# Batch 1's q turned in row pairs, and a new order for every engine, in a fused linear attention and gated unit

## The chip, the core and the metric

The kernel runs on one core of a Trainium2 chip. It is compared by the device time of one execution, in microseconds (us); the times shown are medians of several executions. A core has five engines with a queue of instructions each, which run side by side and wait for each other by semaphores: TensorE (PE in the profile; its weight loads are listed apart as PEld), VectorE (DVE), ScalarE (ACT), GpSimd (POOL) and SyncE (SP), which here only issues transfers (DMAs). TensorE reads SBUF, the core's working memory of 128 partitions, and writes PSUM, eight banks of 2 KB per partition, from which VectorE and ScalarE fetch its results.

## The reference, cut to what matters

```python
def _attn_ref(q, k, v, g_norm):                     # q, k, v: (8, 8, 576, 64)
    kv = np.einsum('bhsd,bhse->bhde', k, v)
    out = np.einsum('bhsd,bhde->bhse', q, kv)
    rms = np.sqrt(np.mean(out * out, axis=-1, keepdims=True) + 1e-06)
    return (out / rms * g_norm).astype(np.float32)

def _moe_ref(x, w_val, conv_w, w_out):              # x: (8, 576, 512)
    ...
    for k in range(K):                              # K = 5, causal
        gate_pre += conv_w[k][None, None, :] * xp[:, k:k + S, :]
    gate = 1.0 / (1.0 + np.exp(-gate_pre))
    val = x @ w_val
    return (gate * val @ w_out).astype(np.float32)
```

The attention's output, heads side by side in 512 channels, is the x of the second part. q, k, v and g_norm are float32; the weights of the second part come as float64 (8 bytes a number) and are narrowed to float32 on the chip.

## The kernel before, in words

Everything is float32. The kernel is a list of steps, the text PLAN at its top. A step is a function name with numbers: `val_product 0 1 1` calls val_product(0, 1, 1), where the first number is mostly the batch. The loop at the end of the file (`for step in PLAN.split(";")`) calls them one after the other, each puts its instructions at the end of its engine's queue, and nothing reorders them: PLAN is the order of all engines at once. What stands behind an @ are the numbers of the buffers that the step takes (`new`, L282): a PSUM bank, or a room in SBUF. A buffer can be taken again once its last reader is done.

One batch of 576 tokens goes through these stages. Chunks are 128 tokens; chunk 4 is the tail of 64.

- k and v are loaded (load_half) and multiplied to one 64x64 kv for each head (kv_product, L475, TensorE), which ScalarE copies out of PSUM (kv_half L485 for batch 0, kv_copy L489 for the others).
- q has to stand with head_dim on the partitions (qT). For batches 2 to 7 VectorE turns it in 32x32 blocks (turn_q, L499). For batches 0 and 1, at the start, TensorE does it: load_q_rows (L366) brings all heads in rows, turn_q_rows turns one chunk into a bank, and sort_q copies the bank to qT. For a batch in PAIRED_Q, turn_q_rows makes one 128x128 transpose of two neighbouring tokens' rows at once (L514), and since the two tokens then lie in different halves of the partitions, sort_q needs four copies of 64 partitions for a chunk (L533; two of batch 0's chunks on VectorE, the rest on ScalarE). For a batch not in PAIRED_Q each token block and head half is its own product with the identity, written straight to its half of the partitions (L520; a float32 product is two instructions), and sort_q is a single copy of 128 partitions on ScalarE (L529).
- q times kv gives the raw output (raw_half L562 for batch 0, raw_pair and raw_tail L550 for the others; raw_pair b c makes chunks c and c-1). Its squares are made by ScalarE (square, L595, L599), summed by VectorE (sums, L606), raised to the power -1/2 by GpSimd (powers, L616), and multiplied in (normalise, batch 0 by VectorE at L625, the others by ScalarE at L635 in eight pieces, one for each head).
- For batches 0 and 1 TensorE turns x (turn_x, L647) and ScalarE copies it to xT (keep_x, L654); from batch 2 on VectorE (turn_blocks) and transfers (move_blocks, L668) do it, but for the tail.
- The gate: ScalarE starts it (gate_start, L679), VectorE adds four taps (gate_tap, L685), ScalarE makes the sigmoid (gate_end, L692). The product x @ w_val is val_product (L697, with keep_val L706) for batches 0 and 1; for the later ones it is val_fast (L746), a scheme with seven products in place of eight that needs sums of x (x_sums) and of weights (val_sums) from VectorE. VectorE multiplies gate and value (gated, L710).
- The output product is fast_product (L837) of the same scheme, with token_sums and weight_sums by VectorE, fast_keep to gather it, and store to write it; the tails go by out_product (L784).

The weights are loaded in four blocks each (stage_weight wval 0 to 3, wout 0 to 3, and cw) and narrowed in seven steps (narrow_weight wval 0 5 is step 5 of block 0): 0, 4, 5, 6 and 7 on VectorE (L399, L411, L416, L421, L425), 1, 2 and 3 on ScalarE (L404, L406, L408). val_product b j needs block j of wval. turn_cw (L450) and keep_cw (L454 to L456, VectorE) bring the convolution's weights and g_norm into columns; start_warm (L463) are products on TensorE whose result nobody reads.

Loads go out on SyncE's queue (batch 0's v and half of its q on ScalarE's).

Of the kernel before, what the change touches and what calls it, by code (L numbers as in the profile page):

```python
# [21 lines left out]
stage_weight cw 0 @ 0; turn_q_rows 0 2 @ 1; turn_q_rows 0 4 @ 2; sort_q 0 2 @ 0; turn_q_rows 0 1 @ 3;  # L22
sort_q 0 4; turn_q_rows 0 0 @ 4; turn_q_rows 0 3 @ 5; sort_q 0 1; start_warm 3 256 @ 6; sort_q 0 3;
load_q_rows 1 1; load_q_rows 1 0; stage_weight wval 3; narrow_weight cw 0 5 @ 0; sort_q 0 0;
kv_product 0 0 @ 0 7; narrow_weight cw 0 6 @ 1; narrow_weight cw 0 0 @ 0; start_warm 1 256 @ 2; kv_half 0 0;
narrow_weight cw 0 1; raw_half 0 1 0 @ 1; narrow_weight cw 0 2; kv_product 0 1; narrow_weight cw 0 3;
narrow_weight cw 0 4; narrow_weight cw 0 7; narrow_weight wval 0 5 @ 2; turn_cw @ 3; kv_half 0 1;
load_half k 2 1 @ 0; raw_half 0 3 0 @ 5; narrow_weight wval 0 0 @ 1; narrow_weight wval 0 6 @ 3;
stage_weight wval 2; narrow_weight wval 0 1; raw_half 0 0 1 @ 6; load_half k 1 0; keep_cw; raw_half 0 3 1;
narrow_weight wval 1 0 @ 0; narrow_weight wval 0 2; stage_weight wout 0 @ 1; raw_half 0 2 0 @ 4;  # L30
narrow_weight wval 1 5 @ 0; stage_weight wout 1 @ 2; square 0 3 @ 0; raw_half 0 2 1;
narrow_weight wval 1 6 @ 1; load_half v 1 0; raw_half 0 4 0 @ 2; narrow_weight wval 0 3; sums 0 3 @ 0 0;
load_half k 1 1; raw_half 0 4 1; square 0 2 @ 1; narrow_weight wval 0 4; raw_half 0 0 0; powers 0 3;
narrow_weight wval 1 1; load_half v 1 1; raw_half 0 1 1; narrow_weight wval 0 7; square 0 4 @ 2;
square 0 0 @ 0; sums 0 2; narrow_weight wval 1 2; sums 0 4; load_half k 2 0 @ 0; normalise 0 3 @ 0;
narrow_weight wval 1 3; powers 0 2; sums 0 0; turn_q_rows 1 3 @ 0; square 0 1 @ 1; narrow_weight wval 1 4;
turn_x 0 3 @ 7; narrow_weight wval 3 0 @ 1; sums 0 1; turn_q_rows 1 0 @ 3; keep_x 0 3; load_half v 2 0 @ 0;
# [192 lines left out]
def kernel(  # L230
# [30 lines left out]
    TURNED_X = 2  # L261
    FAST_VAL = 2
    FAST_OUT = 0
    PAIRED_Q = (0,)
    ACT_SUMS = ()
    ROOTS = {(0, 2): H + H // 2, (0, 1): 2 * H}
    GATES = 3
# [646 lines left out]
```

## Time and profile before

| | us |
|---|---|
| median of three runs | 302.18 |
| the runs | 301.41, 302.18, 302.92 |
| the profiled execution | 300.9 |
| its span, first to last instruction | 299.1 |

The profile is that of one execution. A row of the order in time has the start in us, the length, the engine, the line, the operation, the tile written and those read, the shape of a stationary operand (for TensorE) and of out, and how many such instructions are merged in it; in brackets the time the engine stood idle before it and what ended that. A row of a group has busy time, the mean of one instruction in ns, and the idle time before them. A row of a stretch has its two ends and its length, then for each engine the busy time and the number of instructions, the granted TensorE clock (1.00 is full speed), the share of the sixteen DMA engines' time, and GB/s. Busy times of TensorE overlap, since a matmul starts before the one ahead of it has ended; the distance from one start to the next is what an instruction costs there.

### The profile page before, as it was taken

What the parts mean: (1) busy time and instruction counts of PE and PEld (TensorE: products, weight loads), DVE (VectorE), ACT (ScalarE), POOL (GpSimd) and SP (SyncE); (2) the same over time, 40 slices, a digit from 0 to 9 for tenths busy, and PEclk for the clock granted to TensorE, in tenths of its full rate; (3) what the DMA queues carried; (4) which work ended last, traced back from release to release, by engine and by line L of the source; (5) the groups of instructions that cost most, each with busy time, mean ns of one, the idle gap of its engine ahead of it and who ended that gap; (6) DMA issues with size and microseconds to landing.
All of it is one profiled execution on the core that took longest, in us unless ns stands there. A gap on an engine that the chain in (4) does not pass through costs nothing.

```text
span 299.1 us, 8756 instructions
## 1 busy us (share of the span) xinstructions
PE 289.4 (97%) x3333; PEld 226.9 (76%) x3333; DVE 271.8 (91%) x483; ACT 194.9 (65%) x606; POOL 114.2 (38%) x127
## 2 busy tenths in 40 slices
PE   7979999999999999999999999999999999999993
PEld 4666777778887768778788857788887588888582
DVE  2699999999999999999999999999999999999812
ACT  2888898998767957839773666647579343534230
POOL 3047029437478049309740197400593080000000
PEclk9999999999999999999999999999999999999999
DMA  7999795976588747986886669661650063311344
GB/s 267 380 378 413 271 254 156 307 226 206 150 223 208 231 134 152 289 215 159 259 233 220 175 136 293 195 194 52 158 129 14 22 165 70 99 26 46 77 115 124
DMA packets 32073, 55.51 MB, mean 186 GB/s; under 512 B 6166, under 2 KB 14358, under 8 KB 32032
## 3 DMA queue, kind: packets, MB, share of 16 engines
q1 hardware_dynamic: 29520, 49.76, 56.4%
q0 software_dynamic: 1632, 3.17, 4.8%
q10 hardware_dynamic: 880, 2.03, 1.8%
q8 instruction: 26, 0.43, 0.6%
q14 instruction: 15, 0.12, 0.1%
HBM read 39.21 MB, written 9.44 MB: 163 GB/s over the span
## 4 chain that ended last, share of the span: by engine, by line
PE 82%; DVE 9%; DMA 4%; issue 1%; POOL 1%; SPq 1%; ACT 1%; DVEq 0%
PE bank L837 33%; PE bank L746 28%; PE bank L697 6%; PE bank L550 5%; PE bank L784 5%; DMA y<-in_moe_w_val_dram 4%; PE bank L475 4%; DVE gate L685 3%; DVE ss L606 1%; PE bank L647 1%; POOL rt L616 1%; DVE wexp L411 1%; DVE wval L425 1%; ACT x L635 1%; DVE x L625 1%
## 5 line engine op out<-in xcount | busy, mean ns | idle before, releaser
L685 DVE SCALAR_TENSOR_TENSOR gate<-xT,cwT,gate 128x576 f32<-128x576 f32 x128 | 101.2, 807 | 0.9
L616 POOL TENSOR_TENSOR rt<-ss,mhalf 128x8 f32<-128x8 f32 (+3 forms) x38 | 69.6, 1842 | 59.6 <-DVE ss L606 59.5
L635 ACT ACTIVATE x<-bank,rt 128x64 f32<-128x64 f32 x252 | 55.9, 367 | 8.0 <-POOL rt L616 7.9
L668 POOL DMA_DIRECT2D xT<-y x48 | 26.6, 560 | 71.9 <-PE bank L837 38.0
L837 PE MATMUL bank<-wsum,w 128*128 128x256 f32 x192 | 46.8, 382 | 0.0
L837 PEld LDWEIGHTS bank<-wsum,w 128*128 128x128 f32 x192 | 35.8, 190 | 6.3 <-issue 0.8
L746 PE MATMUL bank<-xs,vsum 128*128 128x288 f32 x144 | 38.5, 407 | 0.0
L697 PE MATMUL bank<-xT,wval 128*128 128x288 f32 x128 | 34.0, 414 | 0.0
L746 PEld LDWEIGHTS bank<-xs,vsum 128*128 128x128 f32 x144 | 27.1, 190 | 7.3 <-DVE gv L753 0.2
L837 PE MATMUL bank<-wout,gv 128*128 128x256 f32 x128 | 32.6, 380 | 0.0
L599 ACT ACTIVATE sq<-bank 128x256 f32<-128x256 f32 (+1 forms) x70 | 21.1, 380 | 12.7 <-PE bank L550 12.5
L697 PEld LDWEIGHTS bank<-xT,wval 128*128 128x128 f32 x128 | 23.4, 190 | 6.4 <-ACT xT L654 0.2
L837 PEld LDWEIGHTS bank<-wout,gv 128*128 128x128 f32 x128 | 24.2, 190 | 3.9
L746 PE MATMUL bank<-xT,wval 128*128 128x288 f32 x96 | 26.4, 408 | 0.0
L606 DVE TENSOR_REDUCE ss<-sq 128x8 f32<-128x520 f32 (+1 forms) x40 | 24.8, 627 | 1.6 <-ACT sq L599 1.6
L679 ACT ACTIVATE gate<-xT,cwT 128x576 f32<-128x576 f32 x32 | 25.8, 813 | 0.5 <-DVE gv L710 0.2
L692 ACT ACTIVATE gate<-gate 128x576 f32<-128x576 f32 x32 | 22.2, 709 | 5.1 <-DVE gate L685 5.1
L847 DVE TENSOR_TENSOR ot<-bank,ot 128x512 f32<-128x512 f32 (+1 forms) x32 | 17.0, 547 | 9.0 <-ACT ot L849 4.9
L710 DVE TENSOR_TENSOR gv<-gv,gate 128x576 f32<-128x576 f32 x32 | 23.5, 750 | 0.9 <-ACT gate L692 0.7
L746 PEld LDWEIGHTS bank<-xT,wval 128*128 128x128 f32 x96 | 18.0, 190 | 4.5 <-ACT x L635 0.2
L550 PEld LDWEIGHTS bank<-kv,qT 64*64 64x64 f32 x1008 | 16.3, 135 | 5.7 <-issue 3.9
L475 PEld LDWEIGHTS bank<-v,k 64*64 64x64 f32 x1008 | 16.0, 135 | 3.8 <-issue 1.6
(93 smaller groups left out, 453.4 us busy)
## 6 DMA issues: line engine op xcount, KB each, us to landing
qs<-in_q_dram SPq DMA_DIRECT2D x96, 140.0 KB, 3.9
out_dram<-ot SPq DMA_DIRECT2D x140, 64.0 KB, 1.9
k<-in_k_dram SPq DMA_DIRECT2D x14, 576.0 KB, 4.3
v<-in_v_dram SPq DMA_DIRECT2D x12, 576.0 KB, 6.0
xT<-y SPq DMA_DIRECT2D x48, 64.0 KB, 2.6
xT<-y POOLq DMA_DIRECT2D x48, 64.0 KB, 2.3
y<-in_moe_w_val_dram SPq DMA_DIRECT2D x4, 512.0 KB, 11.5
w<-in_moe_w_out_dram SPq DMA_DIRECT2D x4, 512.0 KB, 9.6
```

Of the source, the lines that this page charges most:

```text
L475: nc.tensor.matmul(st["kvps", b][s][r * D:(r + 1) * D, i], st["k", b, i][rows, r, cols], st["v", b, i][rows, r, cols], start=(j == 0), sto ...
L550: nc.tensor.matmul(st["raw", b, c][r][cols, to * D:(to + 1) * D], st["qT", b][rows, hp, first:first + D], kvs[b % 2][rows, hp, :], start=T ...
L606: nc.vector.reduce_sum(out=st["ss", b][:, FIRST[c]:FIRST[c] + n], in_=st["sq", b, c][:, 0:n], axis=AX.X)
L616: nc.gpsimd.tensor_tensor(out=st["rt", b][:, which], in0=st["ss", b][:, which], in1=mhalf[:, which], op=ALU.pow)
L635: nc.scalar.activation(out=x[:, to * D:(to + 1) * D], in_=raw[:, h * D:(h + 1) * D], func=AF.Copy, scale=root[:, to:to + 1])
L668: (nc.sync if i % 2 else nc.gpsimd).dma_start(out=xTs[b % 2][i * TB:(i + 1) * TB, :, first:first + P], in_=y[a * TB:(a + 1) * TB, i])
L679: nc.scalar.activation(out=gate[:], in_=xTs[b % 2][:, jt, HALO:SX], func=AF.Copy, scale=cwT[:, K - 1, jt:jt + 1])
L685: nc.vector.scalar_tensor_tensor(out=gate[:], in0=xTs[b % 2][:, jt, tap * TB:tap * TB + S], scalar=cwT[:, tap, jt:jt + 1], in1=gate[:], op ...
L697: nc.tensor.matmul(val[:], wval[:, kc, jt * P:(jt + 1) * P], xTs[b % 2][:, kc, HALO + n * SV:HALO + (n + 1) * SV], start=(kc == 0), stop=( ...
L710: nc.vector.tensor_tensor(out=both, in0=both, in1=st["gate", b, jt][:], op=ALU.mult)
L746: nc.tensor.matmul(st[bank, "val", b, mj][:], weights_[:, k], tokens()[:, k], start=(n in (0, 1, 3) and k == 0), stop=(k == NK // 2 - 1), ...
L837: nc.tensor.matmul(st[bank, i, p], tokens()[:, k], weights_[:, k], start=(n < 2 and k == 0), stop=(k == NK // 2 - 1), skip_group_check=True)
```

## The change

PAIRED_Q takes in batch 1, so that its turn_q_rows and sort_q go the way of batch 0's. All of batch 1's copies in sort_q stay on ScalarE, since only batch 0's chunks 1 and 2 are named for VectorE:

```diff
-    PAIRED_Q = (0,)
+    PAIRED_Q = (0, 1)
```

```python
        for r in range(2):
            for e in range(2):
                (nc.vector.tensor_copy if b == 0 and j in (1, 2) else nc.scalar.copy)(
                    out=qT[r * D:(r + 1) * D, j * HB + e:j * HB + m:2],
                    in_=pq[e * D:(e + 1) * D, r * 2:r * 2 + m // 2])
```

The rest of the change is PLAN: the same 1242 steps in another order, with other buffer numbers. The order was found by a search that scored each candidate by the mean of several runs of a model with disturbed times. The first part of it, up to where the two orders reach batch 1's raw output:

```diff
 load_q_rows 0 1; load_q_rows 0 0; load_half v 0 0 @ 0; load_half k 0 0 @ 0; start_warm 5 256 @ 0;
 load_half v 0 1 @ 0; load_half k 0 1 @ 0; warm_up; stage_weight wval 0; stage_weight wval 1;
-stage_weight cw 0 @ 0; turn_q_rows 0 2 @ 1; turn_q_rows 0 4 @ 2; sort_q 0 2 @ 0; turn_q_rows 0 1 @ 3;
-sort_q 0 4; turn_q_rows 0 0 @ 4; turn_q_rows 0 3 @ 5; sort_q 0 1; start_warm 3 256 @ 6; sort_q 0 3;
-load_q_rows 1 1; load_q_rows 1 0; stage_weight wval 3; narrow_weight cw 0 5 @ 0; sort_q 0 0;
...
-load_half k 2 1 @ 0; raw_half 0 3 0 @ 5; narrow_weight wval 0 0 @ 1; narrow_weight wval 0 6 @ 3;
-stage_weight wval 2; narrow_weight wval 0 1; raw_half 0 0 1 @ 6; load_half k 1 0; keep_cw; raw_half 0 3 1;
-narrow_weight wval 1 0 @ 0; narrow_weight wval 0 2; stage_weight wout 0 @ 1; raw_half 0 2 0 @ 4;
-narrow_weight wval 1 5 @ 0; stage_weight wout 1 @ 2; square 0 3 @ 0; raw_half 0 2 1;
...
-narrow_weight wval 1 1; load_half v 1 1; raw_half 0 1 1; narrow_weight wval 0 7; square 0 4 @ 2;
-square 0 0 @ 0; sums 0 2; narrow_weight wval 1 2; sums 0 4; load_half k 2 0 @ 0; normalise 0 3 @ 0;
-narrow_weight wval 1 3; powers 0 2; sums 0 0; turn_q_rows 1 3 @ 0; square 0 1 @ 1; narrow_weight wval 1 4;
-turn_x 0 3 @ 7; narrow_weight wval 3 0 @ 1; sums 0 1; turn_q_rows 1 0 @ 3; keep_x 0 3; load_half v 2 0 @ 0;
-narrow_weight wval 3 1; normalise 0 2 @ 1; powers 0 1; turn_q_rows 1 1 @ 5; narrow_weight wval 1 7;
-narrow_weight wval 3 2; load_half v 2 1 @ 0; turn_x 0 2 @ 7; normalise 0 4 @ 2; narrow_weight wval 3 3;
-narrow_weight wval 2 5 @ 2; turn_x 0 4 @ 4; narrow_weight wval 2 0 @ 0; turn_q_rows 1 2 @ 2; keep_x 0 4;
-narrow_weight wval 3 5 @ 0; keep_x 0 2; narrow_weight wval 3 6 @ 3; narrow_weight wval 2 1;
-val_product 0 1 1 @ 4; narrow_weight wval 3 4; halo 0; narrow_weight wval 2 2; normalise 0 0 @ 0;
-narrow_weight wval 2 3; normalise 0 1 @ 1; narrow_weight wval 3 7; sort_q 1 0 @ 1; turn_x 0 1 @ 7; sort_q 1 3;
-narrow_weight wout 0 0 @ 1; turn_x 0 0 @ 6; narrow_weight wval 2 4; kv_product 1 0 @ 3 1; keep_x 0 0;
...
+stage_weight cw 0 @ 0; stage_weight wval 2; turn_q_rows 0 0 @ 1; turn_q_rows 0 1 @ 2; turn_q_rows 0 4 @ 3;
+turn_q_rows 0 3 @ 4; sort_q 0 4 @ 0; turn_q_rows 0 2 @ 5; start_warm 3 256 @ 6; load_q_rows 1 0; sort_q 0 0;
+load_q_rows 1 1; stage_weight wval 3; kv_product 0 0 @ 7 0; narrow_weight cw 0 0 @ 0; narrow_weight cw 0 5 @ 0;
...
+narrow_weight wval 1 5 @ 0; raw_half 0 2 1 @ 2; square 0 3 @ 0; narrow_weight wval 1 6 @ 1;
+narrow_weight wval 0 2; turn_cw @ 5; sums 0 3 @ 0 0; raw_half 0 4 0; narrow_weight wval 0 3; raw_half 0 2 0;
+narrow_weight wval 1 0 @ 0; powers 0 3; keep_cw; square 0 4 @ 1; raw_half 0 0 1; narrow_weight wval 0 4;
+square 0 2 @ 2; raw_half 0 1 1 @ 4; sums 0 4; narrow_weight wval 1 1; raw_half 0 1 0; sums 0 2;
+stage_weight wout 2 @ 2; narrow_weight wval 1 2; narrow_weight wval 0 7; powers 0 2; square 0 0 @ 0;
+normalise 0 3 @ 0; load_half k 2 1 @ 0; narrow_weight wval 1 3; narrow_weight wval 2 5 @ 2; turn_x 0 3 @ 0;
+narrow_weight wval 2 0 @ 1; square 0 1 @ 1; sums 0 0; turn_q_rows 1 3 @ 7; narrow_weight wval 2 1;
+load_half k 2 0 @ 0; sums 0 1; turn_q_rows 1 4 @ 5; keep_x 0 3; turn_q_rows 1 1 @ 1; sort_q 1 3 @ 1;
+normalise 0 4 @ 1; powers 0 1; normalise 0 2 @ 2; turn_x 0 4 @ 0; narrow_weight wval 2 6 @ 0; turn_x 0 2 @ 3;
+keep_x 0 4; narrow_weight wval 1 4; turn_q_rows 1 2 @ 2; keep_x 0 2; narrow_weight wval 1 7;
+narrow_weight wval 2 2; val_product 0 0 1 @ 7; narrow_weight wval 3 5 @ 3; sort_q 1 2;
+narrow_weight wout 1 5 @ 2; narrow_weight wval 3 0 @ 0; halo 0; normalise 0 0 @ 0; narrow_weight wval 2 3;
+turn_q_rows 1 0 @ 0; normalise 0 1 @ 1; turn_x 0 0 @ 3; sort_q 1 4; load_q 2 1; narrow_weight wval 2 4;
+turn_x 0 1 @ 2; kv_product 1 0 @ 6 4; narrow_weight wval 2 7; keep_x 0 1; keep_x 0 0;
...
+load_q 2 0; keep_val 0 1 1; gate_tap 0 1 1; kv_copy 1 0; keep_val 0 0 1; keep_val 0 2 1; gate_tap 0 0 1;
+sort_q 1 0; raw_pair 1 3 @ 2 4; gate_tap 0 2 1; narrow_weight wval 3 4; val_product 0 1 0 @ 6;
+load_half v 2 1 @ 0; square 1 2 @ 2; gate_tap 0 3 2; sort_q 1 1; load_half v 2 0 @ 0; sums 1 2 @ 1 1;
+gate_tap 0 1 0; powers 1 2; raw_tail 1 @ 5 7; square 1 3 @ 0; raw_pair 1 1 @ 1 0; narrow_weight wval 3 7;
+keep_val 0 1 0; square 1 4 @ 1; sums 1 3; keep_val 0 0 0; val_product 0 3 1 @ 6; narrow_weight wout 1 3;
+sums 1 4; val_sums 0; square 1 1 @ 2; powers 1 4; gate_tap 0 3 1; normalise 1 2 @ 2;
+narrow_weight wout 2 5 @ 3; val_product 0 3 0 @ 3; powers 1 3; gate_tap 0 3 0; normalise 1 4 @ 0;
+narrow_weight wout 1 4; narrow_weight wout 2 6 @ 2; keep_val 0 3 1; stage_weight wout 0 @ 1; gate_end 0 1;
+turn_x 1 4 @ 5; sums 1 1; turn_x 1 2 @ 7; normalise 1 3 @ 1; val_product 0 2 0 @ 6; turn_q 2 0 @ 0; powers 1 1;
+gate_tap 0 0 0; load_q 2 3; keep_x 1 2; val_sums 1; keep_x 1 4; turn_x 1 3 @ 2; keep_val 0 3 0;
...
```

361 lines of the change are left out of this document (176 added, 185 removed).

## Prediction, made before the changed kernel ran

> **What bounds the kernel now.** I read the page's busy line, its forty slices and the head of its chain of waits first, then the sums over chosen stretches, then the order of single instructions between 15 and 43 us.
>
> ```profile
> PE 289.4 (97%) x3333; PEld 226.9 (76%) x3333; DVE 271.8 (91%) x483; ACT 194.9 (65%) x606; POOL 114.2 (38%) x127
> PE   7979999999999999999999999999999999999993
> DVE  2699999999999999999999999999999999999812
> ACT  2888898998767957839773666647579343534230
> PE 82%; DVE 9%; DMA 4%; issue 1%; POOL 1%; SPq 1%; ACT 1%; DVEq 0%
> ```
>
> TensorE fills nearly every slice, VectorE nearly as many, ScalarE only the first fifteen or so. The sums by stage say it more sharply:
>
> ```profile
> 18.00:22.00 4.00, 2.10 (x25) 1.60 (x23) 3.96 (x8) 3.28 (x7) 3.11 (x2) 1.00 1.08 367
> 22.00:26.00 4.00, 3.45 (x48) 2.74 (x48) 4.00 (x10) 3.05 (x6) 3.54 (x2) 1.00 1.04 412
> 26.00:42.00 16.00, 15.99 (x292) 12.38 (x289) 15.90 (x27) 14.71 (x32) 2.23 (x5) 1.00 0.84 302
> 42.00:50.00 8.00, 7.92 (x161) 5.99 (x160) 8.00 (x15) 6.89 (x26) 6.41 (x4) 1.00 0.59 129
> 50.00:180.00 130.00, 130.00 (x1817) 102.47 (x1818) 127.19 (x222) 96.82 (x336) 67.11 (x72) 1.00 0.76 210
> 180.00:280.00 100.00, 100.00 (x722) 81.08 (x720) 97.70 (x159) 55.66 (x169) 29.38 (x37) 1.00 0.41 110
> 280.00:295.00 15.00, 14.49 (x66) 9.98 (x64) 6.26 (x11) 3.10 (x8) 0.00 (x0) 1.00 0.44 113
> ```
>
> The columns after the length are busy time of TensorE, its weight loads, VectorE, ScalarE and GpSimd. From 26 to 280 us TensorE stands still for 0.09 us in all. So from its first val_product on the time is TensorE's work laid end to end, and there are just two ways to a shorter run: begin that stretch earlier, or put less work into it. Before 26 us it idles for 1.90 and 0.55 us in the first two stretches. VectorE is the near rival: it idles 0.04 us from 18 to 26, 0.10 from 26 to 42, 2.81 from 50 to 180 and 2.30 from 180 to 280.
>
> **TensorE's part of the edit.** The planned order holds the same 1242 steps before and after, counted step by step; only batch 1's turn_q_rows and sort_q change their content.
>
> ```profile
> 6.08 2.18 PE L514 MATMUL bank<-ident,qs 128*128 128x128 f32 x18 [0.60 <-DMA qs<-in_q_dram]
> 19.38 1.09 PE L520 MATMUL bank<-ident,qs 128*64 128x128 f32 x16 [0.86 <-DMA qs<-in_q_dram]
> 21.52 0.66 PE L647 MATMUL bank<-ident,x 128*128 128x128 f32 x4 [1.04 <-DVE x L625]
> 22.10 1.97 PE L520 MATMUL bank<-ident,qs 128*64 128x128 f32 x32
> 24.34 0.63 PE L647 MATMUL bank<-ident,x 128*128 128x128 f32 x4 [0.27 <-DVE x L625]
> 25.61 1.09 PE L520 MATMUL bank<-ident,qs 128*64 128x128 f32 x16
> 26.64 2.21 PE L697 MATMUL bank<-xT,wval 128*128 128x288 f32 x8
> 35.21 0.66 PE L520 MATMUL bank<-ident,qs 128*64 128x128 f32 x8
> 35.80 1.28 PE L475 MATMUL bank<-gv 64*64 64x64 f32 x72
> 42.65 1.16 PE L550 MATMUL bank<-kv,qT 64*64 64x64 f32 x64
> ```
>
> Batch 1's turn takes 72 matmul instructions at L520, 1.09 + 1.97 + 1.09 + 0.66 = 4.81 us. In row pairs it is 18 transposes like batch 0's at L514, 2.18 us: 2.6 us of TensorE's work is gone. But 64 of the 72 stand ahead of the first val_product (26.64 us), where TensorE waits for VectorE anyhow (the 1.04 and 0.27 us waits at L647), so nearly all of that saving falls on idle time. Behind the first val_product, before: turn_q_rows 1 4, 35.80 - 35.21 = 0.59 us. Behind it, after: turn_q_rows 1 0, four transposes, 4/18 of 2.18 = 0.48 us. Everything else behind the first val_product is the same set (two turn_x of batch 0 stand behind it in both). The long stretch shrinks by **0.1 us**, not by 2.6.
>
> **When the stretch begins.** The first val_product needs three turned chunks of batch 0, and these come down VectorE's queue, which starts in earnest when the second weight block lands:
>
> ```profile
> 15.43 0.16 DVE L454 TENSOR_SCALAR gcol<-bank 128x1 f32<-128x1 f32 x1
> 15.89 0.15 DVE L456 TENSOR_SCALAR gcol<-gcol 128x1 f32<-128x1 f32 x1
> 16.45 0.43 DVE L399 TENSOR_SCALAR wexp<-y 128x512 uint32<-128x512 uint32 x1 [0.40 <-DMA y<-in_moe_w_val_dram]
> 21.98 0.68 DVE L411 SCALAR_TENSOR_TENSOR wexp<-y,wexp 128x512 uint32<-128x512 uint32 x1
> 22.58 0.42 DVE L399 TENSOR_SCALAR wexp<-y 128x512 uint32<-128x512 uint32 x1
> 22.91 0.69 DVE L606 TENSOR_REDUCE ss<-sq 128x8 f32<-128x520 f32 x1
> 23.52 0.68 DVE L625 TENSOR_TENSOR x<-bank,rt 128x512 f32<-128x512 f32 x1
> 24.77 0.42 DVE L625 TENSOR_TENSOR x<-bank,rt 128x256 f32<-128x256 f32 x1
> 25.11 0.42 DVE L416 TENSOR_SCALAR ot<-y 128x512 uint32<-128x512 uint32 x1
> ```
>
> Before, normalise 0 2 ends at 24.20 and normalise 0 4 at 25.19; turn_x, keep_x and the first val_product follow 1.45 us later. The loads ahead of block 1 of wval are issued in the same order, so I leave its landing at 16.45. Between that and the end of normalise 0 2 the new order adds keep_cw (15.43 to 16.04, 0.61 us; it ran while VectorE waited for the block, now it comes behind that wait), narrowing steps 5 and 0 of block 2 (0.33 us each, as 22.58 to 22.91) and normalise 0 4 (25.11 - 24.77 = 0.34), and drops step 4 of block 1 (22.58 - 21.98 = 0.60) and step 0 of block 3 (0.33). Net +0.68: normalise 0 2 ends at 24.88, and it is now the later of the two. Then turn_x 0 2 (0.05 + 0.63, the L647 row of 24.34), keep_x 0 2 (0.04 + 0.60) and 0.05 to the first matmul: 26.25. The stretch begins **0.4 us earlier**.
>
> ```profile
> y<-in_moe_w_val_dram SPq DMA_DIRECT2D x4, 512.0 KB, 11.5
> ```
>
> The load of wval block 2, one of these four, now goes out ahead of batch 1's q. At the 412 GB/s of the stretch from 22 to 26 us it is 1.3 us of transfer, so q lands near 19.4 + 1.3 = 20.7; its first user now stands behind turn_x 0 3 (21.5 us or later). Cost nothing; the cover is 0.8 us.
>
> **ScalarE's part.**
>
> ```profile
> L533 ACT COPY qT<-bank 64x256 f32<-64x256 f32 x8 | 2.9, 367 | 0.3 <-PE bank L514 0.2
> L533 ACT COPY qT<-bank 64x128 f32<-64x128 f32 x4 | 1.0, 260 | 3.3 <-PE bank L514 3.3
> L529 ACT COPY qT<-bank 128x512 f32<-128x512 f32 x4 | 2.2, 581 | 0.0
> L529 ACT COPY qT<-bank 128x256 f32<-128x256 f32 x1 | 0.4, 352 | 0.0
> 22.21 0.60 ACT L654 ACTIVATE xT<-bank 128x512 f32<-128x512 f32 x1 [0.89 <-PE bank L647]
> 25.72 0.87 ACT L654 ACTIVATE xT<-bank 128x256 f32<-128x256 f32 x2 [0.46 <-PE bank L647]
> 27.98 0.72 ACT L408 ACTIVATE wexp<-wexp,biases 128x512 uint32<-128x512 uint32 x1
> 41.08 1.57 ACT L599 ACTIVATE sq<-bank 128x128 f32<-128x128 f32 x6
> ```
>
> (The first four columns are groups of instructions, busy time and mean ns; the last four single pieces of the order in time.) Sorting batch 1's q was 5 copies, 2.6 us; now it is 16 of 64x256 and 4 of 64x128, all on ScalarE: 16 x 0.367 + 4 x 0.260 = 6.9 us. **ScalarE gets 4.3 us more** just where it has least room: it idles 1.29 us from 26 to 42 and 1.11 from 42 to 50. What waits first is raw_pair 1 1, which needs sort_q 1 1 and 1 0. Before, TensorE came to it at 42.65, 16.01 us after the first val_product; the same set of steps lies between in the new order but for 0.48 instead of 0.59, so it is wanted at 26.25 + 15.90 = 42.15. On ScalarE, before, the steps from keep_x 0 2 (ended 26.59) to the last square ahead of that point ended at 42.65. New, up to sort_q 1 1: four of the five sorts, 12 x 0.367 + 4 x 0.260 = 5.44 for 2.6, +2.8; seven narrowing steps for nine, -1.4; one square for three, four pieces of 0.26, -1.05; the rest the same. With the start 0.4 earlier and the idle unchanged it ends at 42.65 - 0.4 + 0.35 = 42.6, that is 0.45 late; with ScalarE's idle cut from 1.29 to 0.84, on time. That idle was mostly waiting for TensorE by an engine that was ahead, so part of it goes by itself. **Stall: 0 to 0.45 us, taken 0.3**, since the sorts now stand between two other things TensorE waits for.
>
> VectorE has the same work but 0.6 us of it has moved behind the 16.45 wait, and TensorE comes 0.5 us earlier: together 1.1 us against 5.1 us of idle from 50 to 280. If all that idle stayed, the cost would be the whole 1.1; if the idle gives way, nothing. I count nothing beside ScalarE's 0.3, because a TensorE delayed by one gives the other time: they do not add.
>
> **The sum.** -0.4 (start) - 0.1 (less work) + 0.3 (ScalarE) = -0.2 us: a span of 298.9. The profiled execution took 300.9 us, 1.8 more than its span; the median of the runs is 302.18, 1.3 above it. I keep both offsets: **302.0 us**, no change. Its own range, by the ends above, is -0.5 to +0.6, 301.7 to 302.8.
>
> **Rivals.** *The runs lose less than they did.* The three runs lie at 301.41 to 302.92 while the profiled one took 300.9, with the same work; something in ordinary runs makes waits that this profile does not show. Its start is the likely place: the loads are saturated there (DMA share 1.04 to 1.08). If an order with more room at the early waits lost none of it, the median would fall to the profiled level with the 0.5 us above: 302.18 - 1.28 - 0.5 = 300.4. Against it: at 42 us the new order has less room on ScalarE, not more.
>
> *ScalarE becomes the bound up to 50 us.* After raw_pair 1 1 the remaining squares and the normalise steps of batch 1 have to come before turn_x 1 4, 1 2 and 1 3. Up to the end of normalise 1 3 the new order holds the full 4.3 us of sorting and a normalise more, eight pieces of about 0.2 us, against a narrowing, a keep_x, a square and a gate_end less: about +3.5 us, with some 1.1 us more time. It decides as soon as ScalarE cannot shed nearly all of its 2.4 us idle between 26 and 50. If it keeps it all, TensorE stands still for that long once, and every later step moves: -0.5 + 2.4 = +1.9, 304.1 us. For it: the windows above. Against it: an engine that is late has fewer waits.
>
> *The TensorE clock drops.* In the new order nothing but transposes runs on TensorE between the last raw_half (about 18.5 us) and the first val_product; before, 64 ordinary matmuls lay there. If the gate took that for idleness, the first val_product would run at half speed and lose about its own 2.2 us: -0.5 + 2.2 = +1.7, 303.9 us. Against it: the granted clock was 1.00 from 18 to 22 us although TensorE was busy for only 2.10 of 4.00 us. [...] No row here shows a stretch of only transposes long enough to test it.
>
> **How the numbers follow.** Forecast 0.42, less loss in ordinary runs 0.28, ScalarE 0.18, clock 0.12. What a measurement can tell from no change is about 0.5%, 1.5 us: faster is below 300.7, slower above 303.7. Faster: nearly all of the 0.28 and a little of the forecast's edge, 0.29. Slower: most of 0.18 and 0.12, less those where the loss is only partly paid, 0.24. The same: 0.47. The range reaches from the second case to the ScalarE case, and beyond each by the 0.8 us by which the three runs lie around their median: 299.6 to 304.9.
>
> **What would show it.** Right: the first val_product at 26.2 to 26.4 us, L514 36 instructions and no L520, L533 on ScalarE 32 copies near 10.8 us, TensorE idle of at most 0.5 us from 26 to 280, and the span within 1 us of 299.1. ScalarE's rival shows as a TensorE wait at L550 near 42 or at L647 near 48 to 50, released by ScalarE. The clock's shows as a granted clock under 1.00 near 24 to 30 us. A first val_product before 25.5 or after 27.5 us would prove the VectorE count wrong, and TensorE idle behind 100 us with VectorE named as releaser would prove that its 1.1 us was not free.

## The result, and the profile after

| | before | after |
|---|---|---|
| median | 302.01 us (301.23 to 303.27, 15 runs) | 300.1 us (298.61 to 301.59, 15 runs) |
| ratio, 95% interval | | 0.9945 [0.9926, 0.9964] |
| the profiled execution | 300.9 | 299.81 |
| its span | 299.1 | 298.0 |

The change gains 1.9 us by the medians, 1.7 by the ratio, against a forecast of 0.2. A run over 1.5% above the fastest of its kernel counts as slow and stays out of the ratios (four runs of the fill with transposes, one each of three other kernels below), while medians and ranges hold all runs. First the page after: the busy line, the row of the granted clock by slices (9 is 90% or more), and the head of the chain of waits.

```profile
PE 288.6 (97%) x3279; PEld 226.7 (76%) x3279; DVE 270.9 (91%) x483; ACT 197.2 (66%) x621; POOL 114.9 (39%) x127
PEclk9997999999999999999999999999999999999998
PE 91%; DMA 5%; DVE 2%; SPq 1%; ACT 0%; issue 0%
```

TensorE has 54 instructions fewer and only 0.8 us less busy time than before. New is the 7 in the fourth slice. The stretches after, columns as before (length, then busy time of TensorE, its weight loads, VectorE, ScalarE and GpSimd, granted clock, DMA share, GB/s), first five of the kernel after, and in the second fence the same long stretch before:

```profile
22.00:26.00 4.00, 3.92 (x21) 3.82 (x22) 4.00 (x9) 2.94 (x7) 3.58 (x2) 0.59 1.03 407
42.00:50.00 8.00, 8.00 (x112) 6.48 (x112) 8.00 (x15) 7.97 (x33) 6.69 (x4) 1.00 0.49 177
50.00:180.00 130.00, 130.00 (x1825) 102.18 (x1824) 129.04 (x226) 95.82 (x326) 64.40 (x71) 1.00 0.76 212
180.00:280.00 100.00, 100.00 (x782) 80.70 (x782) 97.49 (x160) 57.02 (x176) 32.44 (x38) 1.00 0.39 103
26.00:280.00 254.00, 253.86 (x2979) 201.65 (x2979) 250.21 (x424) 176.47 (x570) 106.00 (x116) 1.00 0.62 174
```

```profile
26.00:280.00 254.00, 253.90 (x2988) 201.92 (x2984) 248.78 (x419) 174.08 (x558) 105.13 (x116) 1.00 0.62 174
```

Busy time cannot tell the two kernels apart: TensorE is full in both. The order of its instructions can. The start after, and the start of its last group of matmuls after and before:

```profile
22.08 0.66 PE L647 MATMUL bank<-ident,x 128*128 128x128 f32 x4 [2.68 <-DVE x L625]
22.57 2.18 PE L514 MATMUL bank<-ident,qs 128*128 128x128 f32 x10
24.55 1.49 PE L647 MATMUL bank<-ident,x 128*128 128x128 f32 x6
25.83 0.76 PE L514 MATMUL bank<-ident,qs 128*128 128x128 f32 x4
26.72 2.21 PE L697 MATMUL bank<-xT,wval 128*128 128x288 f32 x8
...
292.42 1.03 PE L837 MATMUL bank<-wsum,gv 128*128 128x256 f32 x4
```

```profile
293.46 1.03 PE L837 MATMUL bank<-wsum,gv 128*128 128x256 f32 x4
```

The first val_product starts at 26.72, where it was 26.64: nothing is gained there. From it to the last group it was 293.46 - 26.64 = 266.82 us and is 292.42 - 26.72 = 265.70. The profile's gain of 1.1 us lies in the stretch in which TensorE was counted as busy all the time. Where in it, the same kinds of steps around 50 us show, before and then after:

```profile
49.35 0.94 PE L647 MATMUL bank<-ident,x 128*128 128x128 f32 x4
50.22 1.28 PE L475 MATMUL bank<-v,k 64*64 64x64 f32 x72
51.43 0.66 PE L647 MATMUL bank<-ident,x 128*128 128x128 f32 x4
51.93 1.38 PE L697 MATMUL bank<-xT,wval 128*128 128x288 f32 x5
```

```profile
49.97 0.60 PE L647 MATMUL bank<-ident,x 128*128 128x128 f32 x4
50.50 2.33 PE L475 MATMUL bank<-v,k 64*64 64x64 f32 x144
52.76 1.48 PE L697 MATMUL bank<-xT,wval 128*128 128x288 f32 x5
```

Read the distances between starts. Before, a turn_x of four transposes took 50.22 - 49.35 = 0.87 us, while the next one took 51.93 - 51.43 = 0.50. Of the 0.37 us between them, 0.28 is waiting, most of it booked as busy: the fourth transpose started 0.39 us behind the third instead of 0.11, at 49.96, just after a piece of normalise had ended on ScalarE at 49.91, and the record of the third, which ended at 49.88, covers most of the hole. The rest lies at the step to the next kind of matmul. After, the turn_x shown took 50.50 - 49.97 = 0.53. A kv_product took 51.43 - 50.22 = 1.21 us in front of another kind of matmul; after, two of one batch stand back to back and take 52.76 - 50.50 = 2.26, 1.13 each. Summed by kind from the first val_product to the last group, the distances to the next start fell from 5.20 to 4.63 us for turn_x, from 14.25 to 13.84 for the kv_products of batches 2 to 7 (in 8 groups where there were 12), and from 0.59 to 0.44 for turn_q_rows, as foreseen: together the whole 1.1 us. In the profiles of the two kernels repeated (below) these three fell by as much, 0.60, 0.41 and 0.15, but the rest took 0.6 us more. Counted with one duration for each kind of step, the new order is about 1.2 us further at 70 us in both pairs of profiles, and 1.0 and 0.7 at 270. (These sums and counts are from the starts of all instructions of TensorE; no single view shows them.)

### The profile page after: what moved, and what is told of

It reads as the page before. It is cut to its first block, busy times and chain, and to the rows that moved or that the text cites. A ratio compares the mean times of both kernels' runs of the same rounds, so it can differ in the third digit from the quotient of the medians.

```text
span 298.0 us, 8646 instructions
## 1 busy us (share of the span) xinstructions
PE 288.6 (97%) x3279; PEld 226.7 (76%) x3279; DVE 270.9 (91%) x483; ACT 197.2 (66%) x621; POOL 114.9 (39%) x127
## 4 chain that ended last, share of the span: by engine, by line
PE 91%; DMA 5%; DVE 2%; SPq 1%; ACT 0%; issue 0%
PE bank L837 33%; PE bank L746 28%; PE bank L697 11%; PE bank L550 6%; PE bank L475 5%; PE bank L784 5%; DMA y<-in_moe_w_val_dram 5%; PE bank L647 2%; PE bank L514 1%; DVE ss L606 1%; SPq L347 0%; SPq L381 0%; DVE ot L421 0%; DVE wval L425 0%; DVE x L625 0%; ACT xT L654 0%
## 5 line engine op out<-in xcount | busy, mean ns | idle before, releaser
L616 POOL TENSOR_TENSOR rt<-ss,mhalf 128x8 f32<-128x8 f32 (+3 forms) x38 | 71.1, 1890 | 54.9 <-DVE ss L606 54.7
L697 PE MATMUL bank<-xT,wval 128*128 128x288 f32 x128 | 33.3, 412 | 0.1
L692 ACT ACTIVATE gate<-gate 128x576 f32<-128x576 f32 x32 | 23.2, 741 | 10.2 <-DVE gate L685 10.2
L847 DVE TENSOR_TENSOR ot<-bank,ot 128x256 f32<-128x256 f32 (+1 forms) x32 | 17.3, 549 | 10.1 <-PE bank L837 7.1
L746 PE MATMUL bank<-xT,wval 128*128 128x288 f32 x96 | 26.3, 409 | 0.0
```

The source lines that it names most:

```text
L616: nc.gpsimd.tensor_tensor(out=st["rt", b][:, which], in0=st["ss", b][:, which], in1=mhalf[:, which], op=ALU.pow)
L697: nc.tensor.matmul(val[:], wval[:, kc, jt * P:(jt + 1) * P], xTs[b % 2][:, kc, HALO + n * SV:HALO + (n + 1) * SV], start=(kc == 0), stop=( ...
L746: nc.tensor.matmul(st[bank, "val", b, mj][:], weights_[:, k], tokens()[:, k], start=(n in (0, 1, 3) and k == 0), stop=(k == NK // 2 - 1), ...
```

## Experiments

Ratios are to the kernel before on the same chip in the same session. Twelve kernels ran; the kernel's line numbers shift by up to 13 where lines of its list were added or repacked.

**The half clock.** In the profile after, the clock fell once. From 22 to 26 us it was granted 0.59 of full speed on the mean, and 0.50 in every half microsecond from 23 to 26; at that half speed 0.59 means 0.41 x 4 x 2 = 3.3 us (3.4 with what falls behind 26). The turn_x and turn_q_rows in it took about 0.2 us a transpose (22.57 to 24.55 for ten) instead of 0.11 (22.11 to 23.20 for the same ten in the version with the store, further down, where the clock read 1.000). Ahead of it TensorE had waited 2.68 us for VectorE.

```
-square 0 2 @ 2; raw_half 0 1 1 @ 4; sums 0 4; narrow_weight wval 1 1; raw_half 0 1 0; sums 0 2;
+square 0 2 @ 2; raw_half 0 1 1 @ 4; sums 0 4; narrow_weight wval 1 1; raw_half 0 1 0; start_warm 5 256 @ 7; sums 0 2;
```

> The changed kernel with five idle products (start_warm 5 256, ten matmul instructions, about 2.4 us) put into the 2.68 us in which TensorE waits ahead of turn_x 0 3. Theory (the granted clock): the wait from 19.4 to 22.1 us lets the clock fall to half for 3.4 us, the transposes of 22 to 26 us then run slower and the first val_product begins at 26.72 where 26.25 was worked out. With the wait filled the clock stays at 1.00 throughout in every run, the first val_product begins at 26.2 to 26.4, the span is 297.3 to 297.7, and the median falls 0.5 to 1.0 us below the changed kernel's 300.1, since about half of its runs show a mean clock of 0.991 to 0.994. Rival (the clock costs nothing because only transposes run under it, and the first val_product is held by ScalarE's keep_x or VectorE): clock at 1.00, first val_product still at 26.6 to 26.8, time unchanged within 0.2 us.

Median 300.28 (298.74 to 300.99, 12 runs), ratio 0.9946 [0.9926, 0.9967]; before had 301.37 there. The clock stayed up:

```profile
22.00:26.00 4.00, 3.08 (x24) 2.56 (x24) 4.00 (x9) 3.03 (x8) 3.58 (x2) 1.00 1.04 407
```

and all runs read 0.997 or more, but the ratio is the changed kernel's. So the theory was right on the clock and wrong on the time, and the first val_product came between the two forecasts:

```profile
26.46 2.21 PE L697 MATMUL bank<-xT,wval 128*128 128x288 f32 x8 [0.29 <-ACT xT L654]
```

With pairs, holding the clock is worth nothing that the runs can tell; a difference under some 0.8 us would not show in them. Only transposes ran under the half clock; the profiles put its price at 0.3 to 0.5 us of the start, as shown with the repeats below.

The second form fills the gap with transposes (a new step that turns the identity n times).

```
-raw_half 0 1 0; sums 0 2;
+raw_half 0 1 0; start_turns 20 @ 7; sums 0 2;
```

> The same place filled with 20 transposes of the identity into a spare bank (about 2.2 us) in place of ordinary products. If transposes do not count as activity for the clock, it falls as in the changed kernel (0.5 for 3.4 us near 22 us) and the time is the changed kernel's, 300.1 within 0.3. If they count, the clock stays at 1.00 and the kernel does what the one with ordinary products does. I expect that they count: in the changed kernel's profile the clock came back at 26.15 us after a stretch in which nothing but transposes ran.

Median 301.03 (299.7 to 305.17, 12 runs), ratio 0.9974 [0.9951, 0.9997]. The expectation missed: the clock did not stay up in every run, and the kernel did not do what the one with ordinary products does. Four of the twelve runs read 0.993 or 0.994, and these took 304.24 to 305.17 us. The profile's clock read 1.00 in all of the start, and the first val_product came at 25.54; but its weights had landed early (VectorE began on them at 15.32), and then the clock stayed up in two other kernels without any fill (1.00 from 18 to 30 us, below), so the profile does not say what the transposes did. TensorE then stood still once for no cause that the profile names:

```profile
25.54 1.72 PE L703 MATMUL bank<-xT,wval 128*128 128x288 f32 x6 [0.32 <-ACT xT L660]
...
43.56 0.32 PE L556 MATMUL bank<-kv,qT 64*64 64x64 f32 x2 [1.15 <-issue]
```

**The pairs without the order, and the order without the pairs.**

```
-    PAIRED_Q = (0, 1)
+    PAIRED_Q = (0,)
```

> The new order with batch 1's q turned the old way (72 ordinary matmul instructions, 5 copies). Theory (the gain lies in the order, the pairs alone are worth little): TensorE has 0.6 us more behind the first val_product (turn_q_rows 1 0 with 16 instructions for 4) and 2.1 us more ahead of it, where it waited; ScalarE has 4.3 us less. Span 298.3 to 299.3, median 0.3 to 1.2 us above the changed kernel, still below the kernel before. Rival (the longer sorting on ScalarE holds the changed kernel back at raw_pair 1 1 and turn_x 1 4): it gets faster than the changed kernel by 0.3 us or more.

Median 302.9 (300.54 to 305.24, 12 runs), ratio 1.0038 [1.0007, 1.0069]. Where the clock read 0.996 or more the runs took 300.54 to 302.13, where it read 0.993 or 0.994, 303.67 to 304.59, and one more 305.24. The forecast missed: the kernel is 2.8 us above the changed one by the ratios, not 0.3 to 1.2, and above the kernel before. The profile is one with the low clock:

```profile
23.13 3.69 PE L520 MATMUL bank<-ident,qs 128*64 128x128 f32 x40
...
28.58 1.72 PE L697 MATMUL bank<-xT,wval 128*128 128x288 f32 x6
```

40 products took 3.69 us where 32 took 1.97 at full speed, and the first val_product came 1.86 us later than with pairs. To part the clock from the pairs, the fill of the first experiment was put into this kernel as the last run of the study:

> The new order with the ordinary turn of batch 1 (PAIRED_Q holds batch 0 alone) and with the five filling matmuls of 256 columns behind raw_half 0 1 0, so that the clock stays at 1.0 up to the first val_product. Without the fill this kernel took 1.0038 of before, with runs at 300.5 to 302.1 us where the clock read 0.996 or more and at 303.7 to 305.2 us where it read 0.993 or 0.994. Theory (two causes: at the full clock the pairs earn about 1.1 us in this order, and the half clock costs the ordinary turns 2.9 us more): all runs read 0.997 or more, none above 303 us, the ratio is 0.998 to 1.001, and the first val_product begins 0.5 to 1.3 us behind the filled kernel's with pairs (26.46). Rival (at the full clock the ordinary turns fit just as well, and only the clock made them dear): the ratio of the filled kernel with pairs, 0.993 to 0.997, and a first val_product within 0.3 us of 26.46.

Median 301.16 (300.25 to 301.94, 12 runs), ratio 0.999 [0.9973, 1.0008], the clock at 0.997 or more in all runs. The theory of two causes held:

```profile
22.83 2.40 PE L520 MATMUL bank<-ident,qs 128*64 128x128 f32 x40
...
26.99 2.21 PE L697 MATMUL bank<-xT,wval 128*128 128x288 f32 x8
29.13 1.09 PE L520 MATMUL bank<-ident,qs 128*64 128x128 f32 x16
30.16 1.09 PE L647 MATMUL bank<-ident,x 128*128 128x128 f32 x8
```

The first val_product is 26.99 - 26.46 = 0.53 us behind the filled kernel with pairs, and turn_q_rows 1 0 behind it takes 30.16 - 29.13 = 1.03 instead of 0.44. So at the full clock the new order with ordinary turns is no faster than before that can be told (0.999), and the pairs bring it to 0.9946: 0.44% of 301 us, 1.3 us (0.5 to 2.1 by the two intervals), near the 0.53 + 0.59 that the profile shows. The two profiled executions themselves do not show it whole: their spans are 299.4 with ordinary turns and 299.2 with pairs, since the latter lost more further on.

The pairs in the order of before:

```
-    PAIRED_Q = (0,)
+    PAIRED_Q = (0, 1)
```

> The old order with batch 1's q in row pairs. Theory: TensorE saves only 0.35 us behind the first val_product (two transposes for eight instructions), while ScalarE gets 4.3 us more between 28 and 40 us where it idles 1.3 us; raw_tail 1 (0.43 us of room at sort_q 1 4) and raw_pair 1 1 come late and TensorE stands still for 1.5 to 3 us near 40 to 50 us. Median 1 to 2.5 us above the kernel before. Rival (the pairs are what gains, the order only follows): 0.5 to 2 us below the kernel before.

Median 304.75 (303.81 to 308.89, 6 runs), ratio 1.0102 [1.008, 1.0124]: slower by 3.1 us at the ratio (2.4 to 3.7), the way that the theory forecast and more than its 1 to 2.5. Two windows and the waits:

```profile
22.00:26.00 4.00, 3.41 (x18) 2.82 (x16) 4.00 (x10) 2.84 (x5) 3.54 (x2) 0.52 1.04 411
26.00:30.00 4.00, 3.89 (x13) 2.66 (x12) 3.93 (x8) 3.90 (x9) 2.17 (x5) 0.63 1.04 411
```

```profile
26.85 3.23 PE L697 MATMUL bank<-xT,wval 128*128 128x288 f32 x8
...
32.97 4.15 PE L697 MATMUL bank<-xT,wval 128*128 128x288 f32 x16 [0.81 <-ACT xT L654]
...
39.00 2.21 PE L697 MATMUL bank<-xT,wval 128*128 128x288 f32 x8 [0.46 <-ACT qT L533]
...
43.44 0.48 PE L550 MATMUL bank<-kv,qT 64*64 64x64 f32 x16 [1.14 <-ACT qT L533]
```

Here both things that the prediction feared happen together: the clock is low until the first val_products have run (0.52 and 0.63 in the two windows, 8 matmuls in 3.23 us, where the 8 at 39.00 took 2.21), and ScalarE with its sorts keeps TensorE waiting for 0.81, 0.46 and 1.14 us. The profile's mean clock of 0.987 is the only one so low; the other runs read 0.993 or 0.994, about half of that loss, and but for one of 308.89 took as long (303.81 to 304.98). So the longer half clock is not what most of the 3.1 us is; how they divide between clock and ScalarE was not tested.

**Room on ScalarE in the new order.** The four copies of sort_q 1 1 are made twice.

```
                     in_=pq[e * D:(e + 1) * D, r * 2:r * 2 + m // 2])
+                if (b, j) == (1, 1):
+                    nc.scalar.copy(
+                        out=qT[r * D:(r + 1) * D, j * HB + e:j * HB + m:2],
+                        in_=pq[e * D:(e + 1) * D, r * 2:r * 2 + m // 2])
```

> The changed kernel with the four copies of sort_q 1 1 done twice, 4 x 0.367 = 1.47 us more of ScalarE ahead of raw_pair 1 1. Theory (ScalarE has 0.17 us of room there and none ahead of turn_x 1 4): raw_pair 1 1 begins 1.3 us later, and the time grows by 1.0 to 1.5 us, 0.3 to 0.5%. Rival (TensorE alone bounds this stretch, and the idle time of ScalarE in 42 to 50 us takes it up): 0 to 0.3 us.

Median 302.2 (301.12 to 302.75, 10 runs), ratio 1.0017 [0.9999, 1.0034], 0.7% above the changed kernel's ratio, 2.2 us (1.4 to 3.0 by the two intervals): more than either theory gave, though the interval takes in the upper end of the first. In the profile raw_pair 1 1 went from 42.31 to

```profile
43.83 1.16 PE L554 MATMUL bank<-kv,qT 64*64 64x64 f32 x64 [1.19 <-ACT qT L537]
```

so the whole 1.5 us came through at once, and by 288 us TensorE was 2.6 us behind the first profile of the changed kernel and 2.0 behind the second. ScalarE has no room at this point; the rival that its idle time takes the copies up is out.

**Before or behind 66 us.** At no place have the two orders run through sets that differ by more than 29 of the 1242 steps, so one can be followed up to a point and the other from there. The edits are a cut of PLAN: the first 281 steps of after and then what is left in before's order; the first 290 steps of before (with its ordinary turns) and then what is left in after's order. Where a bank was still taken it was replaced, for example

```
-kv_product 3 0 @ 2 1
+kv_product 3 0 @ 2 3
```

> The new order and the pairs up to 65 us (281 steps), then the remaining steps in the order of before; one bank of kv_product 3 0 is moved, because the one that before's order names is still taken. Theory (the gain is made ahead of 65 us): the profile of before has lost 1.2 us more than the changed one by then, and from there on the two lose about the same, so the ratio is 0.994 to 0.997, not to be told from the changed kernel's. Rival (the new order gains all along, and its gain in the runs lies in the long middle, where it was chosen for disturbed runs): 0.998 to 1.000.

> The other half: before's order and its ordinary turns up to 66 us (290 steps), then the remaining steps in the new order; three banks of val_products are moved. Theory (the gain is made ahead of 65 us): 0.998 to 1.002. Rival (the gain lies behind): 0.994 to 0.997. If each half gives about half, 0.996 to 0.999 in both kernels, both theories fall.

> The new order and the pairs once more in front, now up to 72 us (316 steps), then before's order; the four gates of batch 1 are renamed in that second part so that both orders have the same ones begun at the seam, and gate buffers follow. 8 steps are ahead and 8 behind at the seam, among them only fast_product 0 1 0, raw_tail 2 and val_product 1 3 0 of TensorE. Theory (the gain is made ahead of 66 us): the seam costs under 1 us, the ratio is 0.994 to 0.998, and the profile has lost less than before's all the way behind 72 us, by 0.5 to 1.4 us. Rival (the gain lies behind): 0.998 to 1.002. A jump of the loss between 70 and 85 us would say that the seam does not fit again; then the runs decide nothing.

The first gave 307.34 (305.71 to 308.72, 6 runs), 1.0184 [1.0155, 1.0213]; the third, cut at 316 steps, 304.14 (302.93 to 307.95, 6 runs), 1.0082 [1.0053, 1.0111]. Both miss: the seam does not fit. The first two rows are of the first kernel, the last two of the third:

```profile
66.89 1.28 PE L462 MATMUL bank<-v,k 64*64 64x64 f32 x72 [2.07 <-ACT gv L693]
73.13 1.13 PE L824 MATMUL bank<-wout,gv 128*128 128x256 f32 x4 [0.83 <-ACT x L622]
```

```profile
74.86 1.13 PE L824 MATMUL bank<-wsum,w 128*128 128x256 f32 x4 [0.90 <-ACT kv L476]
...
143.60 1.13 PE L824 MATMUL bank<-wout,w 128*128 128x256 f32 x4 [1.88 <-ACT ot L838]
```

In the third kernel a wait of 1.88 us still comes at 143.60, some 70 us behind the seam; that the seam is its cause is likely, but not shown. The second gave 302.23 (301.26 to 304.24, 12 runs), 1.001 [0.9988, 1.0033], as the theory had it. By the count with one duration for each kind of step its profile lost 0.9 us from 66 to 190 us, where before's two lost 1.3 and 1.8, and then 1.2 us in one hole of the "issue" kind at 195 us. The new order behind 66 us brings nothing by itself that the runs can tell. That the whole gain is made ahead of it was to be shown by the other two, and they did not. The same count on the plain kernels says so for the profiles alone: from the first val_product to 66 us the changed kernel lost 1.1 us less than before in both pairs, and from there to 288 us 0.1 and 0.35 us more.

**Repeats, and a trial of a better version.** The changed kernel and the one before once more, and the fill with one store issued earlier:

> The changed kernel itself, unedited, beside the other three on one chip. Both theories: a ratio near the 0.9945 measured for the change, 0.992 to 0.997, and runs that fall into two groups by the granted clock (0.991 to 0.994 against 0.996 to 1.0), about 1.4 us apart.

> The kernel before, unedited, for a second profile. The first one had a span of 299.1 us where the runs of before have a median near 302, which is 298.9 to 300.2 in span. Theory (that execution was a fast one): the second profile has a span of 299.5 to 300.8, and what it has more lies in waits behind 66 us. Rival (the profile always falls below the runs by this much): 299.1 again, within 0.2.

```
-turn_q 5 3; load_q 6 0;
+turn_q 5 3; store 0 5; load_q 6 0;
...
-turn_blocks 4 0; store 0 5; raw_pair 5 1 @ 7 4;
+turn_blocks 4 0; raw_pair 5 1 @ 7 4;
```

> The changed kernel with five filling matmuls of 256 columns behind raw_half 0 1 0, which hold the clock at 1.0, and with store 0 5 issued ahead of load_q 6 0 on SP's queue instead of behind it, so that the ot buffer of fast_keep 1 0 0 comes free some 1.7 us earlier. Theory (the filled kernel gave back 0.39 us at 147 us because it waits there for that store): the profile no longer shows ScalarE idle for the store ahead of fast_keep 1 0 0, the wait of fast_product 1 0 2 goes, and the time is 0.3 to 0.6 us under the changed kernel's. Rival (the delay only moves to the next wait of the crowded middle, at 193 or 229 us): within 0.3 us of the changed kernel.

The changed kernel repeated: 300.38 (298.39 to 301.73, 12 runs), 0.9943 [0.992, 0.9966], span 298.9. Its runs with a clock of 0.998 or more took 298.39 to 300.14, those with 0.994 or less 299.92 to 301.73. That looks like the clock's doing, but the first experiment held the clock and its runs still spread from 298.74 to 300.99. Before repeated: 301.15 (300.9 to 302.46, 8 runs), 0.9992 [0.9971, 1.0012], span 299.1 again, as the rival had it. But 300.9 is the lowest of these eight runs, so the second profile, too, shows an execution at the fast end; whether that is chance is open. The version with the store: 300.27 (298.24 to 301.51, 12 runs), 0.9947 [0.9923, 0.9971]. Its wait for the store is gone in the profile (first row the filled kernel, second this one), but the runs do not show it, so it is no better version:

```profile
147.07 0.37 ACT L849 COPY ot<-bank 128x256 f32<-128x256 f32 x1 [1.58 <-DMA out_dram<-ot]
```

```profile
144.59 0.37 ACT L849 COPY ot<-bank 128x256 f32<-128x256 f32 x1 [0.83 <-ACT sq L599]
```

Its span, though, was 296.4, the shortest of all. Against the 298.0 of the changed kernel, 1.5 of the 1.6 us are won at the start; against the 299.2 of the filled kernel, 1.2 of 2.8, and the rest was not traced. VectorE's rows at the start, and the first val_product: of the changed kernel, of this version, of before repeated.

```profile
16.49 0.43 DVE L416 TENSOR_SCALAR ot<-y 128x512 uint32<-128x512 uint32 x1 [1.21 <-DMA y<-in_moe_w_val_dram]
```

```profile
15.18 0.43 DVE L416 TENSOR_SCALAR ot<-y 128x512 uint32<-128x512 uint32 x1
...
25.24 2.21 PE L697 MATMUL bank<-xT,wval 128*128 128x288 f32 x8 [0.49 <-ACT xT L654]
```

```profile
16.00 0.42 DVE L399 TENSOR_SCALAR wexp<-y 128x512 uint32<-128x512 uint32 x1
...
26.18 2.21 PE L697 MATMUL bank<-xT,wval 128*128 128x288 f32 x8
```

The second block of wval lands early in some executions and at 16.4 us or later in others, without any edit near it. In the ten profiles that have the new start, VectorE began on it at 15.18 to 15.32 four times, with no wait, and the first val_product came at 25.16 to 25.54; six times it waited 1.2 to 1.5 us, to 16.46 to 16.89, and the first val_product came at 26.46 or later. In two of the four (the kernels cut at 281 and 316 steps) the clock stayed up without any fill, at 1.00 from 18 to 30 us: with the early landing TensorE's wait ahead of turn_x 0 3 was shorter too, 1.45 and 1.44 us against 2.68 to 2.74 in the late ones without fill. Of the late six, four had no fill, and there the clock fell in three. In the fourth, the kernel with the sort made twice, it read 1.00 throughout, though TensorE waited as long:

```profile
16.89 0.43 DVE L416 TENSOR_SCALAR ot<-y 128x512 uint32<-128x512 uint32 x1 [1.51 <-DMA y<-in_moe_w_val_dram]
...
22.48 0.66 PE L651 MATMUL bank<-ident,x 128*128 128x128 f32 x4 [2.72 <-DVE x L629]
...
26.67 2.21 PE L701 MATMUL bank<-xT,wval 128*128 128x288 f32 x8 [0.30 <-ACT xT L658]
```

From VectorE's start on the block to the first val_product it took 26.67 - 16.89 = 9.78 us there, and 26.46 - 16.68 = 9.78 with the fill. Where the clock fell it took 26.72 - 16.49 = 10.23 and, in the repeat, 26.51 - 16.46 = 10.05. So the fall itself costs 0.3 to 0.5 us of the start, and the late landing about 1 us (26.46 and 26.67 at full clock against 25.16 to 25.54): the clock's fall is mostly a companion of the late landing. The runs agree. Of the 27 runs of the changed kernel, the 13 that read 0.996 or more took 299.4 us on the mean and the other 14 took 300.9. If the clock made that difference, the 12 runs with the fill, which all read high, would take 299.4 too; they took 300.0. Before, VectorE reached that point only at 16.00, so the early landing gave it 26.18 instead of 26.64.

## Why the prediction was right in its range and 1.9 us too high

The result is 300.1 us where 302.0 was forecast, inside the range. Of the 1.9 us, 0.9 is the span (298.0 for 298.9) and 1.0 the offset between the profiled execution and the median (0.3 for 1.3). The working of the sum does not earn the hit: the range reaches so low because of a rival, and 300.1 is what the prediction called faster, with a chance of 0.29. Of its signs, the instruction counts came (36 at L514, 32 copies in 8.8 + 2.1 = 10.9 us), and TensorE's idle time of 0.14 us; the first val_product at 26.72 and a span 1.1 under before's lie just outside.

**"From 26 to 280 us TensorE stands still for 0.09 us in all. So ... the time is TensorE's work laid end to end"** is the step that failed. It took busy time for work. The stretch lost 1.1 us (266.82 to 265.70) with the same work but for 0.15 us and the same busy time (253.90 and 253.86 of 254). In the two repeated profiles, first before and then after,

```profile
293.47 1.03 PE L837 MATMUL bank<-wsum,gv 128*128 128x256 f32 x4
```

```profile
26.51 0.75 PE L697 MATMUL bank<-xT,wval 128*128 128x288 f32 x2 [0.29 <-ACT xT L654]
...
293.26 1.03 PE L837 MATMUL bank<-wsum,gv 128*128 128x256 f32 x4
```

it was 293.47 - 26.18 = 267.29 and 293.26 - 26.51 = 266.75, so 0.5: on the mean of both pairs 0.8. The prediction saw "just two ways to a shorter run". The third, which step stands beside which and so how much TensorE waits inside its records, was the one that counted in the profile: 0.57 us at turn_x and 0.41 at the kv_products.

**The edit, -0.1 us behind the first val_product**: right as a difference of the two kernels (0.59 to 0.44). But it is not what the pairs are worth. In the new order ordinary turns cost 0.53 us ahead of the first val_product and 0.59 behind it, 1.3 us in the runs; in the old order the pairs cost 3.1 us. "TensorE waits for VectorE anyhow" held for the old places of the turns only.

**The start, -0.4 us**: VectorE's count was right, normalise 0 2 ended at 24.82 (forecast 24.88). The start came at 26.72, not 26.25, since turn_x 0 2 and turn_q_rows ran at half clock (0.50; six transposes in 25.83 - 24.55 = 1.28 us): with the 9.78 us that the kernels at full clock took, 16.49 gives 26.27, near the forecast. But the landing of the weights, "left at 16.45", is not fixed. The step that was counted as a loss, keep_cw moved behind that wait, lets VectorE come to the block at 15.2 instead of 16.0. With a late landing that costs, with an early one the new order starts 0.6 to 1.0 us sooner than before's 26.18.

**q's landing, nothing**: right; turn_q_rows 1 3 at 22.57 waited for no load.

**ScalarE, +0.3 us**: no stall. sort_q 1 1 ended and raw_pair 1 1's last matmuls went on without a wait:

```profile
40.65 1.49 ACT L533 COPY qT<-bank 64x256 f32<-64x256 f32 x4
```

```profile
42.03 1.41 PE L550 MATMUL bank<-kv,qT 64*64 64x64 f32 x80
```

The first 16 of the 80 are raw_tail 1, 0.28 us; raw_pair 1 1 began at 42.31 (forecast 42.15) and the sort was done at 42.14 (forecast 42.6 with idle unchanged): 0.17 us of room. ScalarE's idle gave way, 0.03 us from 42 to 50 where it had 1.11. The rival of ScalarE as the bound (304.1) was wrong here, but by a narrow margin: 1.5 us more of copies cost 2.2.

**VectorE, nothing**: right; its idle from 50 to 280 fell from 5.11 to 0.96 + 2.51 = 3.47 us and no wait of TensorE came of it that the time shows.

**The clock (303.9)**: the drop came, the price did not: 0.3 to 0.5 us of start in the profiles, nothing in the runs. The clock was back at 26.15, before the first val_product. The 2.2 us that the rival counted no run shows: after's first val_product took 2.21 us, as before's did, and the one that began at the low clock, in the old order with pairs, took 3.23, 1.0 us more. Where ordinary turns ran under it, the price was there: 303.67 to 304.59 us against 300.54 to 302.13.

**The median's offset, 1.3 us kept**: it was 0.3 after, -0.3 in the repeat, and for before itself 0.25 in the repeat, so it says which execution the profile caught as much as what the kernel does. The rival "the runs lose less than they did" gave 300.4 and the result is 300.1; it named the start and its saturated loads (DMA share 1.05 from 18 to 22 us after) as the likely place, and the landing of the second wval block is such a place. That the new order really loses less there is not shown. How often the block lands early in the runs without a profile is not known (if the 13 high clock readings of 27 are the early landings, about every second time), so how the 1.9 us split between the start and the joints stays open: the profiles give 0.8 for the joints, and up to 1.0 for the start in an execution with an early landing.

## What to carry to other kernels

Where an engine is busy 100% of a stretch, compare the distances between the starts of equal steps, not busy time: a wait inside a record (most of 0.28 us at one turn_x here) and a dear neighbour (1.21 us for a kv_product in front of another kind, 1.13 for one of two back to back) both look like work. An edit and the order that it was planned with are priced together: the same edit cost 3.1 us in one order and earned 1.3 in the other, or 2.8 without the fill. And let the engine reach a wait for a load before the latest landing that one profile shows, because another execution may have it earlier: here VectorE went on at 15.2 to 15.3 without a wait in four profiles and at 16.5 to 16.9 in six.

## What was not expected of the hardware

- The granted clock fell after a stretch in which TensorE waited (2.68 us in the first profile of after, 1.48 in that of the old order with pairs), and stayed at half (0.50 in the first, from 22.73 to 26.15) for 3.4 us in the profiles of after and, if it was at half there too, 6.8 us in that of the old order with pairs (0.48 x 4 + 0.37 x 4 = 3.4 us lost, twice that long). In the three profiles that have before's start it never fell (0.999 or more over the execution), with 2.10 of 4.00 us busy from 18 to 22 in the first; after fell with 1.40, the old order with pairs with 1.73, and the kernel with the sort made twice did not fall with 1.76 (22.48 - 2.72 - 18.00). In 11 of the 98 runs of before that went with the experiments it read 0.990 to 0.994, and these were no slower (301.7 us on the mean against 301.9 in the session that has most of them).
- After's clock came back at 26.15 while nothing but transposes ran (22.08 to 26.72), and with the sort made twice it stayed at 1.00 from 19.76 to 26.67 (1.0 over the execution) with nothing but transposes and the wait. So with transposes alone it came back in the one and stayed up in the other. But the old order with pairs did not get the clock back in its first such stretch (21.46 to 26.85, 0.52 from 22 to 26 us), and the fill with transposes did not hold it in four runs of twelve (0.993 or 0.994; where in them it fell is not recorded), where the fill with ordinary products held it in all (0.997 or more): what the clock follows stays open.
- The gap that the profile puts down to "issue", 1.15 and 1.23 us long, came in two kernels amid 64x64 matmuls of one step, with no wait and no transfer named. Its cause was not found.
